# More row maxima among the q projections, a lead stage half as long, and a k-v-gate projection by two products

## The chip, the cores and the metric

The kernel runs on one core of a Trainium2 chip. The metric is the device time of one execution in microseconds; it is 1746.71 us before the change (median of 3 runs, 1746.21 to 1747.7). The engines are PE (matrix products), ACT, DVE and POOL (element-wise work, each with its own queue) and SP, whose queue issues every DMA of this kernel. PE writes to eight PSUM banks, which are named here by their tags: S0 to S4, F0, F1 and V.

## The reference, cut to what matters

```python
a = einsum("bsd,ed->bse", x, dft_hid_re);  b = einsum("bsd,ed->bse", x, dft_hid_im)
y = einsum("ts,bse->bte", dft_seq_re, a) - einsum("ts,bse->bte", dft_seq_im, b)

q = (x @ wq).reshape(B, S, 32, 20).transpose(0, 2, 1, 3)      # 32 heads of 20
k = x @ wk;  v = x @ wv                                       # one k and v for all heads
p = softmax(einsum("bhqd,bkd->bhqk", q, k) * 20 ** -0.5)
o = einsum("bhqk,bkd->bhqd", p, v)  ->  (S, 640) @ wo

g = sigmoid((x * gate_w).sum(-1))
out = g * y + (1 - g) * o
```

S is 2048 and D is 640, all in float32. To hold that precision the kernel splits most operands into a high part (rounded to fp32r) and the rest, the low part, and adds three products: high by high, high by low, low by high.

## The kernel before, in words

**Projection stage.** x comes in four blocks n = 0 to 3 of 512 tokens. Of each block, five chunks c of 128 channels are split into xh (ACT) and xl (DVE). Two things are projected: kv, 41 columns of k, v and the gate (`kv_mm`, `kv_out`), and q, in five tiles m of 128 columns, 15 matmuls of 512 columns each (`q_mm`, `q_out`). `q_out` copies the high part qh from PSUM (ACT), subtracts to get ql (DVE) and sends both to DRAM (qh_d, ql_d); three buffers each rotate. `kv_out` does the same with k and sends it six times into ks; `kv_turn` transposes v and the gate. Block 0 runs chunk by chunk, since the weights wq come in chunks too; blocks 1 to 3 run tile by tile. In block 3, four half maxima follow each of the tiles m = 0 to 3.

**A half maximum** ("a half") is one matmul of 128 queries by 512 keys for one head into a bank (`a_unit`, PE `a<-ks,qs`) and one maximum over the keys from that bank (DVE `mx<-a`). It needs the rows qs of its head, which are read back from qh_d and ql_d (`load_qs`), and ks. 64 half maxima finish a pair of heads, over 1024 queries; the sum over keys can start only after that.

**Lead stage.** 240 puts (a put is one step of a DFT product, on both halves of PE at once) make the first 16 groups of the hidden DFT (`ab`, 15 puts each), with 72 half maxima between them. They use the weights w0 (real part), wb and w1 (imaginary part), each loaded as `wraw` and split on POOL (`load_w`, `split_w`), and tiles of x, loaded as `xraw` (`load_x`) and split by ACT (`xh<-xraw`) and POOL (`xl<-xraw`) in `split_x`. All raw tiles of these two kinds go through one ring of two buffers (`raw_tile`).

**Loop.** 256 rounds. Each has 8 exponentials on ACT (`pt<-b`) with their score matmuls b, 16 matmuls av, in rounds that need it 8 half maxima, and a number of DFT puts. Plan AB15 has 15 puts of the hidden DFT (rounds 0 to 47), Y16 has 16 puts of the sequence DFT (rounds 48 to 191, six products), Y12 has 12 (rounds 192 to 223, the seventh product), and then come output groups and the end. A short tail follows.

**What sets the order.** Orders on PE, ACT, DVE and POOL are those in which the program is written. The DMAs on SP are put in order by a scheduler at build time, and SP then takes them strictly one after the other: a DMA that has to wait holds all that are behind it.

Of the kernel before, what the change touches and what calls it, by code (L numbers as in the profile page):

```python
# [8 lines left out]
F32 = mybir.dt.float32  # L9
# [8 lines left out]
P = 128  # L18
# [15 lines left out]
def kernel(  # L34
# [66 lines left out]
    gate = const.tile([P, NT], F32, name="gate")  # L101
    omg = const.tile([P, NT], F32, name="omg")

    nc.gpsimd.memset(ks.bitcast(F32), 1.0)
    nc.gpsimd.memset(vsb, 1.0)

    nc.scalar.activation(gate, ident[:, :NT], AF.Exp)

# [47 lines left out]
    for t in mxr:
# [69 lines left out]
    mx = {}  # L226
    QB = NT // 2
    UV = 4 * QB

    def a_unit(u, hh, tag="A"):  # L230

        v, r = divmod(u, UV)
        qb, c = divmod(r, 4)
        if r == 0 and v not in mx:
            mx[v] = qsp.tile([P, 2, QB, 4], F32, tag=f"mx{v % 2}", name="mx", bufs=1)
        b = 64 * hh
        ps = bank(tag, f"a_{u}_{hh}")
        nc.tensor.matmul(  # L238
            ps,
            qs[v][b : b + 60, qb * P : (qb + 1) * P],  # L240
            ks[b : b + 60, c * ROW : (c + 1) * ROW],
            start=True,
            stop=True,
        )
        nc.vector.tensor_reduce(mx[v][:, hh, qb, c : c + 1], ps, axis=AX.X, op=ALU.max)  # L245
# [74 lines left out]
    with ExitStack() as c1:  # L320
        w1 = c1.enter_context(tc.tile_pool(name="w1", bufs=1, side="right"))
        x1 = c1.enter_context(tc.tile_pool(name="x1", bufs=2, side="right"))
        rot = Rot(["B", "V", "F", "B", "F", "A", "A", "A"])
        kvg = w1.tile([P, KC, 41], F32, name="kvg")
        kvgh = w1.tile([P, KC, P], F32R, name="kvgh")
        kvgl = w1.tile([P, KC, P], F32R, name="kvgl")
        nc.gpsimd.memset(kvgh.bitcast(F32), 0.0)
        nc.gpsimd.memset(kvgl.bitcast(F32), 0.0)
        wqh = w1.tile([P, KC, D], F32R, name="wqh")
        wql = w1.tile([P, KC, D], F32R, name="wql")  # L330
        wq_v = wq.rearrange("(c p) n -> p c n", p=P)
        xs, xsp = {}, {}

        def load_x1(n, c):
            if n < 4:
                if c == 0:
                    xs[n] = x1.tile([P, KC, ROW], F32, name="xr")
                move(xs[n][:, c], xT_v[:, c, n * ROW : (n + 1) * ROW])

        def split_x1(n, c):  # L340
            if n < 4:
                if c == 0:
                    xh = x1.tile([P, KC, ROW], F32R, name="xh")
                    xl = x1.tile([P, KC, ROW], F32R, name="xl")
                    xsp[n] = (xh, xl)
                xh, xl = xsp[n]
                split(xs[n][:, c], xh[:, c], xl[:, c])

        def q_mm(ps, n, m, c):
            ms = slice(m * P, (m + 1) * P)  # L350
            xh, xl = xsp[n]
            mm3(ps, wqh[:, c, ms], wql[:, c, ms], xh[:, c], xl[:, c], KC, c)

        def q_out(ps, n, m):
            ms, ts = slice(m * P, (m + 1) * P), slice(n * ROW, (n + 1) * ROW)
            qh = x1.tile([P, ROW], F32R, name="qh", bufs=3)
            ql = x1.tile([P, ROW], F32R, name="ql", bufs=3)
            nc.scalar.activation(qh, ps, AF.Copy)
            nc.vector.tensor_tensor(ql, ps, qh.bitcast(F32), op=ALU.subtract)
            move(qh_d[ms, ts], qh)  # L360
            move(ql_d[ms, ts], ql)

        def kv_mm(ps, n, c):
            xh, xl = xsp[n]
            mm3(ps, kvgh[:, c], kvgl[:, c], xh[:, c], xl[:, c], KC, c)

        def kv_out(ps, n):
            ts = slice(n * ROW, (n + 1) * ROW)
            kvT = x1.tile([41, ROW], F32, name="kvT")
            kh = x1.tile([DH, ROW], F32R, name="kh")  # L370
            kl = x1.tile([DH, ROW], F32R, name="kl")
            nc.scalar.activation(kvT, ps[:41], AF.Copy)
            nc.scalar.activation(kh, ps[:DH], AF.Copy)
            nc.vector.tensor_tensor(kl, ps[:DH], kh.bitcast(F32), op=ALU.subtract)
            for r0 in (0, 64):
                move(ks[r0 : r0 + 20, ts], kh)
                move(ks[r0 + 20 : r0 + 40, ts], kl)
                move(ks[r0 + 40 : r0 + 60, ts], kh)
            return kvT

        def kv_turn(kvT, n, rot):
            ps = rot(f"kvt_{n}")
            for j in range(4):
                nc.tensor.transpose(
                    ps[:, 64 * j : 64 * j + 41], kvT[:, j * P : (j + 1) * P], ident[:41, :41]
                )
            pv = ps.rearrange("p (j c) -> p j c", c=64)[:, :4]
            ns = slice(4 * n, 4 * n + 4)
            nc.scalar.activation(vsb[:, ns, :DH], pv[:, :, DH : 2 * DH], AF.Copy)
            nc.vector.tensor_copy(  # L390
                gz[:, ns].rearrange("p (j o) -> p j o", o=1), pv[:, :, 2 * DH : 2 * DH + 1]
            )


        def gate_out():
            nc.vector.tensor_scalar_max(gz, gz, -87.0)
            nc.scalar.activation(omg, gz, AF.Exp, scale=-1.0)
            nc.vector.tensor_scalar_add(omg, omg, 1.0)
            nc.vector.reciprocal(gate, omg)
            nc.vector.tensor_scalar(omg, gate, -1.0, 1.0, op0=ALU.mult, op1=ALU.add)  # L400

        load_x1(0, 0)
        move(kvg, wkvg.rearrange("(c p) n -> p c n", p=P))
        pkv = rot("kv_0")
        pq = [rot(f"q_0_{m}") for m in range(KC)]
        for c in range(KC):
            if c:
                load_x1(0, c)
            raw = w1.tile([P, D], F32, name="wraw", bufs=2)
            move(raw, wq_v[:, c])  # L410
            split_x1(0, c)
            if c == 0:
                split(kvg, kvgh[:, :, :41], kvgl[:, :, :41])
            split(raw, wqh[:, c], wql[:, c])
            kv_mm(pkv, 0, c)
            for m in range(KC):
                q_mm(pq[m], 0, m, c)
        for c in range(KC):
            load_x1(1, c)
        for c in range(KC):  # L420
            split_x1(1, c)
        kvT = kv_out(pkv, 0)
        for m in range(KC):
            q_out(pq[m], 0, m)
        for n in range(1, 4):
            for c in range(KC):
                load_x1(n + 1, c)
            if n == 3:
                rot = Rot(["F1", "V", "S0", "F0", "F1", "V", "S0", "F0"])
            pkv = rot(f"kv_{n}")  # L430
            for c in range(KC):
                kv_mm(pkv, n, c)
            kv_turn(kvT, n - 1, rot)
            kvT = kv_out(pkv, n)
            if n == 3:
                load_qs(0)
                for k in range(2):
                    load_x(k)
                for k in range(2):
                    split_x(k)  # L440
                load_x(2)
            for m in range(KC):
                ps = rot(f"q_{n}_{m}")
                for c in range(KC):
                    q_mm(ps, n, m, c)
                split_x1(n + 1, m)
                q_out(ps, n, m)
                if n == 3 and m < KC - 1:
                    for z in range(4):
                        a_half(z % 2, f"S{1 + z}")  # L450
                    if m == 1:
                        kv_turn(kvT, 3, rot)
                        gate_out()
            if n < 3:
                load_w(n - 1, 0)
                split_w(n - 1)
# [563 lines left out]

    LEAD = 12
    NL = 2 * (UV + LEAD)
    KL = 15 * 2 * SJ
    done = first = 2 * state[0]
    for n in range(1, KL + 1):
        y_put(1)
# [10 lines left out]
    stage["loop"] = True  # L1037

    ROUNDS = [(p, qh, kk) for qh in range(2) for p in range(NPAIR) for kk in range(NT // 2)]
    NAB = 3 * 2 * SJ  # L1040
    Y3 = 48

    NO = len(ROUNDS) - NT * 2

    def plan_of(n):
        if n < NAB or NO <= n < NO + NT:
            return AB15
        if n < NAB + 3 * Y3:
            return Y16
        if n >= len(ROUNDS) - 2:  # L1050
            return N0
        return Y12 if state[1] < NA else N12
# [95 lines left out]
```

## Time and profile before

| | us |
|---|---|
| median of three runs | 1746.71 |
| the profiled execution | 1745.61 |
| its span | 1743.8 |
| projection stage (0 to 99.9) | 99.9 |
| lead stage (99.9 to 145.6) | 45.7 |
| loop, 256 rounds (145.6 to 1719.8) | 1574.2 |
| tail | 24.0 |

The granted clock of the profiled execution is 0.998. PE is busy for 99% of the span, DVE 78%, ACT 73%, POOL 63%. A window row gives a stretch's length, then each engine's busy time and instructions, the granted PE clock, the DMA share and GB/s. A timeline row gives start, length, engine, source line, operation, out<-in, shapes and count, and in brackets how long the engine sat idle before and what ended that.

### The profile page before, as it was taken

To read this page: it belongs to the slowest core of one execution; us is meant where nothing else is said; L and a number is where in the kernel's file an instruction comes from. 1 tells how busy PE (TensorE), PEld (TensorE's weight loads), DVE (VectorE), ACT (ScalarE), POOL (GpSimd) and SP (SyncE) were. 2 spreads that over 40 slices of the span, in tenths; PEclk is the share of its full clock that TensorE was granted. 3 is DMA by queue.
4 is the path that set the end of the run, shared out by engine and by line. 5 is a ranking of instruction groups with operands and counts; after the bars stand their busy time and mean duration, and the time that the engine had idled before them with its cause. 6 is when DMAs were issued, how large, how long until landed. Compare 5 with 4: busy or idle time off the path is not lost.

```text
span 1743.8 us, 43691 instructions
## 1 busy us (share of the span) xinstructions
PE 1723.9 (99%) x16754; PEld 1230.0 (71%) x16754; DVE 1363.0 (78%) x2285; ACT 1270.6 (73%) x2556; POOL 1095.9 (63%) x910
## 2 busy tenths in 40 slices
PE   8999999999999999999999999999999999999997
PEld 6797777777777677777777777777777666667664
DVE  4498888888887888888888888888888888888823
ACT  3337887878767777777777777777777777788895
POOL 4056563333788555577778888888877453357784
PEclk9999999999999999999999999999999999999999
DMA  7652232222777533466667775555555232234332
GB/s 247 189 168 88 67 109 86 67 71 71 236 222 237 181 104 114 136 194 231 222 200 226 243 229 173 194 188 175 172 168 155 88 102 73 63 109 123 102 92 84
DMA packets 181322, 261.49 MB, mean 150 GB/s; under 512 B 35636, under 2 KB 136244, under 8 KB 181112
## 3 DMA queue, kind: packets, MB, share of 16 engines
q1 hardware_dynamic: 181112, 258.70, 47.3%
q8 instruction: 131, 2.15, 0.5%
q14 instruction: 79, 0.65, 0.1%
HBM read 184.42 MB, written 76.99 MB: 150 GB/s over the span
## 4 chain that ended last, share of the span: by engine, by line
PE 92%; DVE 3%; DMA 2%; SPq 1%; issue 1%; ACT 1%; POOL 0%; POOLq 0%; DVEq 0%; ACTq 0%
PE av L934 27%; PE y_p L742 19%; PE b L922 19%; PE a L238 15%; PE ab L742 6%; PE oo L742 3%; DVE mx L245 2%; SPq L113 1%; PE q L121 1%; PE q L123 1%; PE q L122 1%; DMA wraw<-in_wq_dram 1%; DMA qh_d<-qh 0%; DVE xl L117 0%; DMA xr<-in_xT_dram 0%
## 5 line engine op out<-in xcount | busy, mean ns | idle before, releaser
L245 DVE TENSOR_REDUCE mx<-a 128x1 f32<-128x512 f32 x2048 | 1277.6, 684 | 260.7 <-PE a L238 234.1
L930 ACT ACTIVATE pt<-b 128x512 f32<-128x512 f32 x2048 | 1073.1, 605 | 337.2 <-PE a L238 269.3
L922 PE MATMUL b<-qs,ks 62*128 62x512 f32 x2048 | 762.0, 413 | 3.4 <-ACT pt L930 1.4
L238 PE MATMUL a<-ks,qs 60*128 60x512 f32 x2048 | 719.2, 409 | 0.5 <-DVE mx L245 0.4
L742 PE MATMUL y_p<-tb,ch 64*128 64x320 f32 x3584 | 633.4, 306 | 0.0
L922 PEld LDWEIGHTS b<-qs,ks 62*128 62x128 f32 x2048 | 346.3, 185 | 225.2 <-DVE mx L245 155.2
L934 PE MATMUL av<-pt,vsb 128*32 128x512 f32 x4096 | 492.3, 598 | 0.0
L742 PEld LDWEIGHTS y_p<-tb,ch 64*128 64x128 f32 x3584 | 480.0, 185 | 9.0
L742 PE MATMUL y_p<-tb,cl 64*128 64x320 f32 x1792 | 444.9, 306 | 0.0
L238 PEld LDWEIGHTS a<-ks,qs 60*128 60x128 f32 x2048 | 350.6, 185 | 7.3 <-issue 1.1
L784 POOL TENSOR_TENSOR yt<-yt,yu 128x320 f32<-128x320 f32 x86 | 74.8, 870 | 336.3 <-ACT yu L779 307.0
L742 PEld LDWEIGHTS y_p<-tb,cl 64*128 64x128 f32 x1792 | 274.6, 185 | 5.7
L503 POOL TENSOR_TENSOR cl<-craw,ch 128x1024 fp32r<-128x1024 f32 x112 | 268.0, 2393 | 9.0
L934 PEld LDWEIGHTS av<-pt,vsb 128*32 128x32 f32 x4096 | 107.0, 109 | 224.8 <-issue 215.5
L784 POOL TENSOR_TENSOR abt<-abt,abu 128x320 f32<-128x320 f32 x64 | 55.8, 872 | 183.3 <-ACT abu L779 175.8
L497 POOL TENSOR_TENSOR craw<-craw 128x1024 f32<-128x1024 f32 x64 | 153.8, 2403 | 0.0
L502 POOL CAST ch<-craw 128x1024 fp32r<-128x1024 f32 x112 | 116.3, 1038 | 13.8 <-DMA braw<-b_d 7.4
L742 PE MATMUL oo<-wo,osp 64*128 64x320 f32 x816 | 92.9, 307 | 0.0
L742 PEld LDWEIGHTS oo<-wo,osp 64*128 64x128 f32 x816 | 87.4, 185 | 1.6
L529 POOL TENSOR_TENSOR tb<-braw,tb 128x320 fp32r<-128x320 f32 x80 | 68.4, 876 | 0.0
L742 PE MATMUL ab<-wbh,xh 64*128 64x320 f32 x256 | 59.0, 307 | 0.0
L742 PE MATMUL ab<-wbh,xl 64*128 64x320 f32 x256 | 58.3, 305 | 0.0
(138 smaller groups left out, 1614.2 us busy)
## 6 DMA issues: line engine op xcount, KB each, us to landing
craw<-in_cre_dram SPq DMA_DIRECT2D x80, 512.0 KB
craw<-in_cim_dram SPq DMA_DIRECT2D x64, 512.0 KB
s_d<-craw SPq DMA_DIRECT2D x32, 512.0 KB
craw<-s_d SPq DMA_DIRECT2D x32, 512.0 KB
braw<-b_d SPq DMA_DIRECT2D x80, 160.0 KB
xraw<-in_xT_dram SPq DMA_DIRECT2D x32, 320.0 KB
qs<-qh_d SPq DMA_DIRECT2D x128, 80.0 KB
b_d<-abt SPq DMA_DIRECT2D x64, 160.0 KB
```

The costliest lines, as they stand in the source:

```text
L113: nc.sync.dma_start(words(dst), words(src))
L238: nc.tensor.matmul(ps, qs[v][b : b + 60, qb * P : (qb + 1) * P], ks[b : b + 60, c * ROW : (c + 1) * ROW], start=True, stop=True,)
L245: nc.vector.tensor_reduce(mx[v][:, hh, qb, c : c + 1], ps, axis=AX.X, op=ALU.max)
L497: nc.gpsimd.tensor_tensor(raw[0], raw[0], raw[1], op=how)
L502: nc.gpsimd.tensor_copy(h, raw[0])
L503: nc.gpsimd.tensor_tensor(l, raw[0], h.bitcast(F32), op=ALU.subtract)
L529: nc.gpsimd.tensor_tensor(t[:, 1], raw, t[:, 0].bitcast(F32), op=ALU.subtract)
L742: nc.tensor.matmul(ps, w, x, start=start, stop=stop)
L784: nc.gpsimd.tensor_tensor(t0, t0, t1, op=ALU.add)
L922: nc.tensor.matmul(ps, ks[b : b + 62, kc * P : (kc + 1) * P], qs[NPAIR * (qc // 2) + p][b : b + 62, (qc % 2) * ROW : (qc % 2 + 1) * ROW], ...
L930: nc.scalar.activation(t, ps, AF.Exp, scale=SCALE)
L934: nc.tensor.matmul(ps[32 * g : 32 * g + 32, :], vsb[:, kc, :], t, start=first, stop=last)
```

## The change

- **k, v and gate by two products.** The high and the low part of the weights stand side by side in one stationary tile kvgs (columns 0 to 40 and 64 to 104). One matmul per chunk by xh makes high by high and low by high at once, in two groups of PSUM rows; a second one by xl uses the first 41 columns. `kv_out` adds the two groups: ACT copies the low rows (kvl), DVE adds (kvT), ACT makes kh and DVE kl.
- **Start.** Nine matmuls of 128 columns on the identity are issued before anything else on PE. The memsets of ks and vsb come after that of kvgs.
- **xl of blocks 2 and 3** is subtracted on POOL and no longer on DVE.
- **Banks.** From block 1 on, the projections rotate over four banks (F1, V, S0, F0), so that S1 to S4 are free for the half maxima.
- **Half maxima.** qs of the first pair of heads is loaded block by block (`load_qs0`), the half maxima go in key order (`EARLY`), and four follow each of the tiles m = 2, 3 of block 1 and all five of blocks 2 and 3: 48 rather than 16 in the projection stage.
- **Lead and loop.** The lead stage has 120 puts (8 groups) and 40 half maxima. The other 8 groups go into the loop: AB15 in rounds 0 to 55, Y16 in rounds 56 to 223, and no Y12 for the seventh product.

```diff
+    warm = bank("S4", "warm")
+    for _ in range(9):
+        nc.tensor.matmul(warm[:, :P], ident, ident, start=True, stop=True)
...
+    EARLY = [(qb, 0) for qb in range(4)] + [(qb, 0) for qb in range(4, QB)]
+    EARLY += [(qb, c) for c in range(1, 4) for qb in range(QB)]
...
-        rot = Rot(["B", "V", "F", "B", "F", "A", "A", "A"])
+        rot = Rot(["S1", "S0", "F0", "S2", "S3", "S4", "F1", "V", "S0", "F0"])
...
-                split(xs[n][:, c], xh[:, c], xl[:, c])
+                nc.scalar.activation(xh[:, c], xs[n][:, c], AF.Copy)
+                (nc.gpsimd if n > 1 else nc.vector).tensor_tensor(
+                    xl[:, c], xs[n][:, c], xh[:, c].bitcast(F32), op=ALU.subtract
+                )
...
-            mm3(ps, kvgh[:, c], kvgl[:, c], xh[:, c], xl[:, c], KC, c)
+            end = c == KC - 1
+            for high in (not end, end):
+                m, x = (105, xh) if high else (41, xl)
+                nc.tensor.matmul(ps[:m], kvgs[:, c, :m], x[:, c], start=(c == 0 and high), stop=(end and high))
...
-            nc.scalar.activation(kvT, ps[:41], AF.Copy)
-            nc.scalar.activation(kh, ps[:DH], AF.Copy)
-            nc.vector.tensor_tensor(kl, ps[:DH], kh.bitcast(F32), op=ALU.subtract)
+            nc.scalar.activation(kvl, ps[64:105], AF.Copy)
+            nc.vector.tensor_tensor(kvT, ps[:41], kvl, op=ALU.add)
+            nc.scalar.activation(kh, kvT[:DH], AF.Copy)
+            nc.vector.tensor_tensor(kl, kvT[:DH], kh.bitcast(F32), op=ALU.subtract)
...
+        load_qs0(0)
+        rot = Rot(["F1", "V", "S0", "F0"])
+        slots = {1: (2, 3), 2: range(KC), 3: range(KC)}
...
-            if n == 3:
-                rot = Rot(["F1", "V", "S0", "F0", "F1", "V", "S0", "F0"])
...
-                load_qs(0)
...
-                if n == 3 and m < KC - 1:
+                if (n, m) == (1, 0):
+                    load_qs0(1)
+                if m in slots[n]:
                     for z in range(4):
                         a_half(z % 2, f"S{1 + z}")
...
-    KL = 15 * 2 * SJ
+    KL = 15 * SJ
...
-    NAB = 3 * 2 * SJ
-    Y3 = 48
+    NAB = 7 * SJ
+    NY = 3 * SJ * len(PRODUCTS)
```

The queue of SP changes although no line says so. Before, the loads of the imaginary weights (wiT) and of the first two x tiles of the lead stage (xraw) stand among the loads of the first blocks (xr), ahead of everything that block 0 sends:

```order
L113 DMA wraw<-in_wiT_dram 128x3x320
L113 DMA wraw<-in_wiT_dram 128x2x320
L113 DMA wraw<-in_wq_dram 128x640
L113 DMA xr<-in_xT_dram 128x512 x5
L113 DMA xraw<-in_xT_dram 128x5x128 x2
L113 DMA xr<-in_xT_dram 128x512 x5
L113 DMA ks<-kh 20x512
```

Now they stand behind the last q tile that block 2 sends, and the ks of block 3:

```order
L114 DMA qh_d<-qh 128x512
L114 DMA ql_d<-ql 128x512
L114 DMA wraw<-in_wiT_dram 128x3x320
L114 DMA wraw<-in_wiT_dram 128x2x320
L114 DMA ks<-kh 20x512
L114 DMA ks<-kl 20x512
L114 DMA ks<-kh 20x512 x2
L114 DMA ks<-kl 20x512
L114 DMA ks<-kh 20x512
L114 DMA xraw<-in_xT_dram 128x5x128 x2
L114 DMA qs_119<-qh_d 20x1024 x2
```

What moved are two transfers of weights and two of x, past some 55 other DMAs.

On POOL the splits of both sets of weights stood together, ahead of the x tiles:

```order
L200 CAST w0h<-wraw 128x960
L201 TENSOR_TENSOR w0l<-wraw,w0h 128x960
L200 CAST wbh_500<-wraw 128x640
L201 TENSOR_TENSOR wbl_501<-wraw,wbh_500 128x640
L200 CAST w1h<-wraw 128x960
L201 TENSOR_TENSOR w1l<-wraw,w1h 128x960
L200 CAST wbh<-wraw 128x640
L201 TENSOR_TENSOR wbl<-wraw,wbh 128x640
L316 TENSOR_TENSOR xl<-xraw,xh 128x640 x2
```

Now the subtractions of blocks 2 and 3 stand around the first set:

```order
L361 TENSOR_TENSOR xl<-xr,xh 128x512 x5
L211 CAST w0h<-wraw 128x960
L212 TENSOR_TENSOR w0l<-wraw,w0h 128x960
L211 CAST wbh_539<-wraw 128x640
L212 TENSOR_TENSOR wbl_540<-wraw,wbh_539 128x640
L361 TENSOR_TENSOR xl<-xr,xh 128x512 x5
L211 CAST w1h<-wraw 128x960
L212 TENSOR_TENSOR w1l<-wraw,w1h 128x960
L211 CAST wbh<-wraw 128x640
L212 TENSOR_TENSOR wbl<-wraw,wbh 128x640
L329 TENSOR_TENSOR xl<-xraw,xh 128x640 x2
```

The order of the weights and the x tiles among themselves is the same; five subtractions are ahead of the first set and five between the two.

On ACT, at the start of block 3, the two copies `xh<-xraw` stand ahead of the copies qh of that block's q tiles, as they did before:

```order
L372 ACTIVATE kvT<-kv_683 41x512
L373 ACTIVATE kh<-kv_683 20x512
L315 ACTIVATE xh<-xraw 128x640 x2
L358 ACTIVATE qh<-q_0_740 128x512
L358 ACTIVATE qh<-q_1_775 128x512
```

and now:

```order
L394 ACTIVATE kh<-kvT 20x512
L328 ACTIVATE xh<-xraw 128x640 x2
L374 ACTIVATE qh<-q_0_833 128x512
L374 ACTIVATE qh<-q_1_867 128x512
L410 ACTIVATE vsb<-kvt_901 128x4x20
```

Here nothing moved but the copy of k, which now follows the sum kvT on DVE; q_0 and q_1 are the first two q tiles of block 3.

More of the change, by code (lines that the diff above doesn't have):

```diff
@@ L102 @@
     omg = const.tile([P, NT], F32, name="omg")
-    nc.gpsimd.memset(ks.bitcast(F32), 1.0)
-    nc.gpsimd.memset(vsb, 1.0)
+    warm = bank("S4", "warm")
+    for _ in range(9):
+        nc.tensor.matmul(warm[:, :P], ident, ident, start=True, stop=True)
     nc.scalar.activation(gate, ident[:, :NT], AF.Exp)
@@ L153, in load_qs, with load_qs0 @@
             move(t[b + 40 : b + 60], ql_d[r, ts])
+    def load_qs0(n):
+        if n == 0:
+            qs[0] = qbuf[0]
+        ts = slice(n * ROW, (n + 1) * ROW)
+        for hh in range(2):
+            r = slice(hh * DH, (hh + 1) * DH)
+            for k, src in enumerate((qh_d, qh_d, ql_d)):
+                b = 64 * hh + 20 * k
+                move(qs[0][b : b + 20, ts], src[r, ts])
     mxr = [qsp.tile([P, 32], F32, name=f"mxr{i}") for i in range(2)]
@@ L228 @@
     UV = 4 * QB
+    EARLY = [(qb, 0) for qb in range(4)] + [(qb, 0) for qb in range(4, QB)]
+    EARLY += [(qb, c) for c in range(1, 4) for qb in range(QB)]
     def a_unit(u, hh, tag="A"):
         v, r = divmod(u, UV)
-        qb, c = divmod(r, 4)
+        qb, c = EARLY[r] if v == 0 else divmod(r, 4)
         if r == 0 and v not in mx:
@@ L322 @@
         x1 = c1.enter_context(tc.tile_pool(name="x1", bufs=2, side="right"))
-        rot = Rot(["B", "V", "F", "B", "F", "A", "A", "A"])
+        rot = Rot(["S1", "S0", "F0", "S2", "S3", "S4", "F1", "V", "S0", "F0"])
         kvg = w1.tile([P, KC, 41], F32, name="kvg")
[L325 to L328, printed above, removed]
+        kvgs = w1.tile([P, KC, P], F32R, name="kvgs")
+        nc.gpsimd.memset(kvgs.bitcast(F32), 0.0)
+        nc.gpsimd.memset(ks.bitcast(F32), 1.0)
+        nc.gpsimd.memset(vsb, 1.0)
         wqh = w1.tile([P, KC, D], F32R, name="wqh")
@@ L369, in kv_out @@
             kvT = x1.tile([41, ROW], F32, name="kvT")
+            kvl = x1.tile([41, ROW], F32, name="kvl", bufs=1)
             kh = x1.tile([DH, ROW], F32R, name="kh")
             kl = x1.tile([DH, ROW], F32R, name="kl")
-            nc.scalar.activation(kvT, ps[:41], AF.Copy)
-            nc.scalar.activation(kh, ps[:DH], AF.Copy)
-            nc.vector.tensor_tensor(kl, ps[:DH], kh.bitcast(F32), op=ALU.subtract)
+            nc.scalar.activation(kvl, ps[64:105], AF.Copy)
+            nc.vector.tensor_tensor(kvT, ps[:41], kvl, op=ALU.add)
+            nc.scalar.activation(kh, kvT[:DH], AF.Copy)
+            nc.vector.tensor_tensor(kl, kvT[:DH], kh.bitcast(F32), op=ALU.subtract)
             for r0 in (0, 64):
@@ L410 @@
             move(raw, wq_v[:, c])
+            if c == 0:
+                nc.vector.tensor_copy(kvgs[:, :, :41], kvg)
+                nc.vector.tensor_tensor(
+                    kvgs[:, :, 64:105], kvg, kvgs[:, :, :41].bitcast(F32), op=ALU.subtract
+                )
             split_x1(0, c)
-            if c == 0:
-                split(kvg, kvgh[:, :, :41], kvgl[:, :, :41])
             split(raw, wqh[:, c], wql[:, c])
@@ L447 @@
                 q_out(ps, n, m)
-                if n == 3 and m < KC - 1:
+                if (n, m) == (1, 0):
+                    load_qs0(1)
+                if m in slots[n]:
                     for z in range(4):
                         a_half(z % 2, f"S{1 + z}")
-                    if m == 1:
-                        kv_turn(kvT, 3, rot)
-                        gate_out()
+                if (n, m) == (3, 1):
+                    kv_turn(kvT, 3, rot)
+                    gate_out()
             if n < 3:
@@ L1047, in plan_of @@
             return AB15
-        if n < NAB + 3 * Y3:
+        if n < NAB + NY:
             return Y16
```

## The prediction, made before the changed kernel had run

> **What bounds the kernel now.** I read the busy shares first, then the span by stages (columns: length, then PE, PEld, DVE, ACT and POOL busy), then the stages' timelines.
>
> ```profile
> PE 1723.9 (99%) x16754; PEld 1230.0 (71%) x16754; DVE 1363.0 (78%) x2285; ACT 1270.6 (73%) x2556; POOL 1095.9 (63%) x910
> ...
> 0.00:30.70 30.70, 23.86 (x91) 18.48 (x92) 14.54 (x15) 12.73 (x23) 17.49 (x24) 1.00 0.78 250
> ...
> 74.50:99.90 25.40, 25.40 (x116) 18.33 (x114) 14.70 (x28) 5.88 (x12) 3.08 (x2) 1.00 0.47 151
> 99.90:145.60 45.70, 45.18 (x558) 44.53 (x559) 44.62 (x77) 23.08 (x56) 36.34 (x37) 1.00 0.48 147
> ```
>
> The average says PE. In the projection of blocks 1 to 3 that holds: PE has no gap, DVE has room. In the lead stage PE and DVE are both full (45.18 and 44.62 of 45.70). DVE's row there is one unbroken run of maxima, 28.96 / 48 = 0.603 us each, so PE's fullness is partly a pace that DVE sets:
>
> ```profile
> 101.33 28.96 DVE L245 TENSOR_REDUCE mx<-a 128x1 f32<-128x512 f32 x48
> ```
>
> The loop is read by its exponentials, 8 to a round, in the stretches of plan AB15, Y16 and Y12:
>
> ```profile
> 145.60:440.80 295.20, 203.66 (x384) 1.00 0.26 78
> 440.80:1345.40 904.60, 597.62 (x1152) 1.00 0.60 191
> 1345.40:1539.20 193.80, 137.79 (x256) 1.00 0.27 81
> ```
>
> A round of AB15 takes 295.20 / 48 = 6.150 us, of Y16 904.60 / 144 = 6.282, of Y12 193.80 / 32 = 6.056. Four more puts cost 0.22 us: in a round a put is cheap, since the round's maxima and exponentials are there anyway.
>
> **Loop.** 32 rounds of Y12 become 8 of AB15 and 24 of Y16: 8 × 6.150 + 24 × 6.282 − 32 × 6.056 = **+6.2**. Bounds 5 to 8, the upper one if the longer Y16 part, which moves 191 GB/s, meets its own transfers.
>
> **Start of the projection.** Block 0 waits for weights: PE stood 5.71 us at the start and 0.28 + 0.84 in chunk 2.
>
> ```profile
> 5.71 0.79 PE L121 MATMUL kv<-xh,kvgh 128*128 128x512 f32 x1 [5.71 <-ACT kvgh L116]
> ...
> 10.57 0.40 PE L123 MATMUL q<-xh,wql 128*128 128x512 f32 x1
> ...
> 17.54 0.50 PE L121 MATMUL q<-xh,wqh 128*128 128x512 f32 x1 [0.28 <-ACT wqh L116]
> ...
> 19.12 0.50 PE L123 MATMUL q<-xh,wql 128*128 128x512 f32 x1 [0.84 <-DVE wql L117]
> ...
> 16.75 0.74 ACT L116 ACTIVATE wqh<-wraw 128x640 fp32r<-128x640 f32 x1 [7.13 <-DMA wraw<-in_wq_dram]
> ...
> 17.52 1.54 DVE L117 TENSOR_TENSOR wql<-wraw,wqh 128x640 fp32r<-128x640 f32 x1 [7.17 <-ACT wqh L116]
> ```
>
> The nine warm-up matmuls and the missing kv product shorten chunks 0 and 1, but chunk 2 still starts when its wq has landed and is split. That load is one place earlier on SP, ahead of 320 KB that take 1.3 us at the window's 250 GB/s; I take 0.9. The subtraction wql, 1.54 us while POOL splits weights, has POOL idle beside it now; I take half its time off, 0.7. Chunks 3 and 4 save two matmuls of 0.233: **−2.1** (−1 to −3). The pace of the first eleven matmuls, (10.57 − 5.71) / 11 = 0.44, is covered by that wait.
>
> **Products of k, v and gate.** A 512-column matmul starts every (77.90 − 74.64) / 14 = 0.233 us; blocks 1 to 3 save 15: **−3.5**. The extra DVE addition per block has cover where DVE idles (14.70 busy of 25.40).
>
> ```profile
> 74.64 0.39 PE L121 MATMUL kv<-xh,kvgh 128*128 128x512 f32 x1
> ...
> 77.90 0.39 PE L123 MATMUL kv<-xh,kvgl 128*128 128x512 f32 x1
> ...
> 82.28 0.73 PE L238 MATMUL a<-ks,qs 60*128 60x512 f32 x4
> ...
> 86.64 0.73 PE L238 MATMUL a<-ks,qs 60*128 60x512 f32 x4
> ...
> 83.63 2.47 DVE L245 TENSOR_REDUCE mx<-a 128x1 f32<-128x512 f32 x4
> ```
>
> **Half maxima among the q tiles.** A tile with four half maxima takes 86.64 − 82.28 = 4.36 us, one without 15 × 0.233 = 3.50; eight more tiles have them: 8 × 0.86 = **+6.9**. On DVE each costs 2.47 us for the four maxima and 0.69 for ql (`75.47`, below), 3.2 of 4.36 us, so it keeps up; the ten subtractions that leave for POOL find it empty between the splits of weights.
>
> **Lead stage.** 72 maxima become 40: 32 × 0.603 = **−19.3**. PE's side is lower: 120 puts and 40 half maxima are half and 56% of what filled 45.18 us, about 24, against DVE's 26.4. If PE were the sole bound it would be −21.
>
> **Block 1.** Four banks rotate now, so q tile 2 takes the bank of kv_1, which is free when ACT and DVE have made kvl and kvT. Those stand behind the last q tiles of block 0, and these wait for buffers, that is for qh_d to land:
>
> ```profile
> 31.57 2.24 SPq L113 DMA_DIRECT2D xr<-in_xT_dram  x5
> 33.91 0.91 SPq L113 DMA_DIRECT2D ks<-kh  x1
> ...
> 38.84 0.42 SPq L113 DMA_DIRECT2D qh_d<-qh  x1
> ...
> 41.44 0.60 ACT L358 ACTIVATE qh<-q 128x512 fp32r<-128x512 f32 x1 [10.24 <-DMA qh_d<-qh]
> 43.45 0.60 ACT L358 ACTIVATE qh<-q 128x512 fp32r<-128x512 f32 x1 [1.41 <-DMA qh_d<-qh]
> ```
>
> Before, nothing on PE needed that in time. Now PE wants the bank when block 0, kv_1 and two tiles are through: 30.7 − 2.1 + 10 × 0.233 + 0.4 + 7.0 = 38.3. On SP the loads of xraw and of the last x block no longer stand ahead, so I put the first ks at 27.9 and qh_d at 27.9 + 4.93 = 32.8; the landings follow 2.6 and 4.6 us later as in the rows, then 0.6 (qh), 0.7 (ql), 0.6 and 0.7 (kvl, kvT): 39.8 to 40. Stall 1.5, and 0.3 for the first half maxima behind the round trip of qs: **+1.8** (0 to 5).
>
> **Block 3.** This is the term that decides. The raw tiles use a ring of two, and the order is wiT, wiT, xraw, xraw. Before, wiT left SP at 18.41 and xraw at 26.06, some 50 us ahead of need; ACT copied xraw without a wait.
>
> ```profile
> 18.41 3.62 SPq L113 DMA_DIRECT2D wraw<-in_wiT_dram  x2
> ...
> 26.06 2.93 SPq L113 DMA_DIRECT2D xraw<-in_xT_dram  x2
> ...
> 22.12 1.02 POOL L200 CAST w1h<-wraw 128x960 fp32r<-128x960 f32 x1 [0.51 <-DMA wraw<-in_wiT_dram]
> ...
> 26.55 2.04 POOL L201 TENSOR_TENSOR wbl<-wraw,wbh 128x640 fp32r<-128x640 f32 x1
> ...
> 74.40 0.40 PE L123 MATMUL q<-xh,wql 128*128 128x512 f32 x1
> ...
> 79.78 1.35 ACT L315 ACTIVATE xh<-xraw 128x640 fp32r<-128x640 f32 x2
> 82.39 0.60 ACT L358 ACTIVATE qh<-q 128x512 fp32r<-128x512 f32 x1 [1.26 <-PE q L123]
> ...
> 75.47 0.69 DVE L359 TENSOR_TENSOR ql<-q,qh 128x512 fp32r<-128x512 f32 x1 [2.21 <-ACT qh L358]
> ```
>
> Now wiT stands behind ql_d of block 2's last tile. Let T be the start of that tile's last matmul (74.40 in the rows). ql ends 1.8 later, so wiT leaves at T + 2.1. By the rows it is used 22.12 − 18.41 = 3.7 after that, and POOL ends the four steps of the splits (26.55 + 2.04) − 22.12 = 6.5 later: T + 12.3. Only then is the second buffer free and the second xraw leaves; with the same 3.7 it lands at T + 16.1. ACT waits for it with `xh<-xraw`, and behind that stand the copies qh of block 3. So xh ends at T + 16.9, qh of tile 0 at 17.4, ql at 18.1, its four maxima at 20.6. The half maxima of tile 1 need the banks of those of tile 0, one after the other, so their last goes at T + 20.6. PE wants it at (86.64 − 74.40) − 5 × 0.233 + 0.86 + 3 × 0.15 = T + 12.4: **+8.2** (0 to 9). PE idles for about 6 of these.
>
> **Clock.** What PE loses after a gap is seen at the end of the kernel: after 1.96 us of idling (and 0.21 a little later) the pace goes from (1726.80 − 1724.74) / 14 = 0.147 to (1734.26 − 1731.06) / 12 = 0.267 for 12 matmuls, 1.4 us.
>
> ```profile
> 1724.74 0.31 PE L121 MATMUL o_late<-wo,osp 128*128 128x320 f32 x1
> ...
> 1726.80 0.31 PE L123 MATMUL o_late<-wo,osp 128*128 128x320 f32 x1
> 1729.07 0.42 PE L121 MATMUL o<-wl,osp 128*128 128x320 f32 x1 [1.96 <-ACT osp L980]
> ...
> 1731.06 0.47 PE L121 MATMUL o<-wl,osp 128*128 128x320 f32 x1
> ...
> 1734.26 0.33 PE L121 MATMUL o<-wl,osp 128*128 128x320 f32 x1
> ```
>
> I take **+1.4** after block 3's gap (0 to 2.3, what the start's eleven slow matmuls lost, 11 × 0.21). [...]
>
> **Sum.** To the first exponential −2.1 − 3.5 + 6.9 − 19.3 + 1.8 + 8.2 + 1.4 = −6.6, with the loop's +6.2 **−0.4**. The profiled execution takes 1745.61 (span 1743.8 and 1.8 around it), 1.1 below the median, so this is 1745.2 for it and about **1746** for the median.
>
> **Rivals.**
> - *The hold in block 3 is absent or short.* For it: the chain goes through five queues, and each step is taken at the pace of another place. Against it: order and ring are fixed, and the price has two transfers and four splits in a row. Without the stall and its clock, −0.4 − 9.6 = −10.0: 1736.7. With half of it, 1741.5.
> - *Slower, by kv_1's bank.* If qh_d leaves SP no earlier than before, at 38.84, kvT comes at 45.5 to 46 and PE stalls some 7.4 rather than 1.5: 1752.2. It makes the kernel slower by over 0.2% from qh_d at about 37. For it: SP is strictly in order and had the x loads of 2.24 us ahead. Against it: the kv result is ready 2 us sooner.
> - *The loop takes the puts worse than the rows say* (upper bound 8): 1748, still within 0.2%.
> - *The change doesn't do what it says:* if two products don't shorten kv because a 105-row product takes longer, −3.5 goes: 1749.8. Nothing speaks for it; the cost in the rows goes by the columns.
>
> **How the numbers follow.** 0.2% is 3.5 us, about what a measurement of this kernel tells from no change. Forecast 0.50; hold absent 0.15, halved 0.13; bank 0.10; loop 0.08; kv 0.04. The forecast's own range is 1742 to 1750. Faster by over 0.2% (below 1743.2): 0.15 + 0.10 of the halved case + 0.09 of the forecast = 0.34. Slower (above 1750.2): 0.09 of the bank + 0.04 of the forecast + 0.03 of the last two = 0.16. Same: 0.50. The range goes from 1737.5 to 1750.5, which leaves some 0.1 at each end.
>
> **What would show it.** In the changed profile: first exponential near 139, or near 130 if the hold is absent; `xh<-xraw` at the start of block 3 idle about 10 us before it on the DMA of xraw; PE idle about 6 us before a half maximum on `mx`; a stall of 1 to 2 us in block 1; maxima at 0.6 us through a lead stage of about 27 us; loop rounds at 6.15 and 6.28. The forecast is wrong if ACT reaches qh of block 3 without waiting, or if the rounds change pace.

## The result, and the profile after

| | before | changed |
|---|---|---|
| median, us (20 runs each, same chip) | 1746.45 | 1750.71 |
| lowest to highest | 1744.56 to 1748.04 | 1748.04 to 1753.89 |
| profiled: span | 1743.8 | 1749.4 |
| profiled: first put of the lead | 99.94 | 113.16 |
| profiled: first exponential | 145.64 | 142.07 |
| profiled: loop (first exponential to the last round's end) | 1574.2 | 1583.4 |

The changed kernel is **slower**, by 0.23%: ratio 1.0023, interval 1.0016 to 1.003. The forecast was no change, 1746 in a range of 1737.5 to 1750.5.

The changed kernel in four windows, which hold most of block 1, of block 2, of block 3 and the lead (columns as before). The first matmuls of blocks 1, 2 and 3 stand at 28.81, 53.69 and 78.24:

```profile
28.50:52.00 23.50, 21.42 (x93) 15.19 (x92) 8.80 (x15) 8.01 (x16) 5.15 (x5) 1.00 0.75 218
52.00:76.00 24.00, 24.00 (x107) 16.81 (x107) 16.50 (x28) 7.05 (x13) 13.07 (x10) 1.00 0.64 191
76.00:110.00 34.00, 26.96 (x111) 18.21 (x110) 16.61 (x32) 6.27 (x12) 8.74 (x6) 0.85 0.55 155
112.40:142.10 29.70, 26.88 (x288) 25.45 (x286) 27.84 (x49) 11.66 (x29) 17.14 (x18) 0.94 0.33 104
```

The window from 76 to 110 shows the loss: PE lacks 7 us of 34 and its granted clock is 0.85. Its timeline, engine by engine along the forecast's chain (SP, POOL, ACT, DVE, PE):

```profile
79.45 0.98 SPq L114 DMA_DIRECT2D wraw<-in_wiT_dram  x2
...
88.23 1.81 SPq L114 DMA_DIRECT2D xraw<-in_xT_dram  x2
...
83.81 1.19 POOL L211 CAST w1h<-wraw 128x960 fp32r<-128x960 f32 x1 [8.01 <-DMA wraw<-in_wiT_dram]
...
88.08 1.56 POOL L212 TENSOR_TENSOR wbl<-wraw,wbh 128x640 fp32r<-128x640 f32 x1
...
91.51 0.74 ACT L328 ACTIVATE xh<-xraw 128x640 fp32r<-128x640 f32 x1 [8.07 <-DMA xraw<-in_xT_dram]
93.51 0.74 ACT L328 ACTIVATE xh<-xraw 128x640 fp32r<-128x640 f32 x1 [1.27 <-DMA xraw<-in_xT_dram]
94.27 1.09 ACT L374 ACTIVATE qh<-q 128x512 fp32r<-128x512 f32 x2
...
94.90 0.69 DVE L375 TENSOR_TENSOR ql<-q,qh 128x512 fp32r<-128x512 f32 x1 [10.75 <-ACT qh L374]
...
96.25 2.58 PE L251 MATMUL a<-ks,qs 60*128 60x512 f32 x4 [7.04 <-DVE mx L258]
...
99.35 0.63 PE L123 MATMUL q<-xl,wqh 128*128 128x512 f32 x1
...
101.91 0.41 PE L123 MATMUL q<-xl,wqh 128*128 128x512 f32 x1
```

wiT leaves late, the splits follow, the second xraw leaves when wbl's split has ended, ACT waits 8.07 + 1.27 us for the two, and PE idles 7.04 us for a bank. Then, from 99.35 to 101.91, six matmuls run at 0.43. In the loop, two rounds stand out: round 60 takes 6.86 us and round 63 takes 9.07, by the first exponentials of consecutive rounds. In round 63 PE waits for the transfer that adds the maxima to qs. The maxima m are complete at 518.9, and m_d, which sends them, leaves SP at 535.31:

```profile
540.08 0.47 PE L948 MATMUL b<-qs,ks 62*128 62x512 f32 x1 [2.76 <-DMA qs<-m_d]
...
518.70 0.22 DVE L273 TENSOR_REDUCE m<-m 128x32 fp32r<-128x64 f32 x1
...
530.50 1.75 SPq L114 DMA_DIRECT2D braw<-b_d  x4
...
535.31 1.22 SPq L114 DMA_DIRECT2D m_d<-m  x2
538.35 0.55 SPq L114 DMA_DIRECT2D qs<-m_d  x2
```

### The profile page after: what moved, and what is told of

It reads as the page before. It is cut to its first block, busy times and chain, and to the rows that moved or that the text cites. A ratio compares the mean times of both kernels' runs of the same rounds, so it can differ in the third digit from the quotient of the medians.

```text
span 1749.4 us, 43682 instructions
## 1 busy us (share of the span) xinstructions
PE 1717.4 (98%) x16752; PEld 1223.0 (70%) x16752; DVE 1359.8 (78%) x2280; ACT 1261.8 (72%) x2543; POOL 1113.6 (64%) x931
## 4 chain that ended last, share of the span: by engine, by line
PE 93%; DVE 2%; DMA 2%; ACT 1%; POOL 1%; SPq 0%; issue 0%; POOLq 0%; DVEq 0%; ACTq 0%
PE av L960 27%; PE y_p L768 19%; PE b L948 19%; PE a L251 15%; PE ab L768 7%; PE oo L768 3%; DVE mx L258 1%; PE q L122 1%; PE q L124 1%; PE q L123 1%; SPq L114 0%; ACT pt L956 0%; DMA wraw<-in_wq_dram 0%; DMA xr<-in_xT_dram 0%; DMA wraw<-in_wiT_dram 0%
## 5 line engine op out<-in xcount | busy, mean ns | idle before, releaser
L948 PE MATMUL b<-qs,ks 62*128 62x512 f32 x2048 | 750.2, 408 | 6.5 <-DMA qs<-m_d 2.8
L251 PE MATMUL a<-ks,qs 60*128 60x512 f32 x2048 | 704.6, 409 | 10.6 <-DVE mx L258 9.4
```

The lines of the kernel that those rows point to most:

```text
L251: nc.tensor.matmul(ps, qs[v][b : b + 60, qb * P : (qb + 1) * P], ks[b : b + 60, c * ROW : (c + 1) * ROW], start=True, stop=True,)
L948: nc.tensor.matmul(ps, ks[b : b + 62, kc * P : (kc + 1) * P], qs[NPAIR * (qc // 2) + p][b : b + 62, (qc % 2) * ROW : (qc % 2 + 1) * ROW], ...
```

## Experiments

My theory after the comparison: the hold in block 3 costs about 9.6 us as forecast; the lead is DVE's chain of maxima and gave less than forecast; the loop costs the forecast's 6 us, and a further wait for `qs<-m_d`. Ratios are against the kernel before, on the same chip.

**e1: the hold taken away.**

```diff
-                for k in range(2):
-                    split_x(k)
-                load_x(2)
...
+                if (n, m) == (3, 3):
+                    for k in range(2):
+                        split_x(k)
+                    load_x(2)
```

> The changed kernel, but the first two x tiles of the lead stage are split after q tile 3 of block 3 rather than ahead of tile 0, so that ACT's copies qh no longer stand behind the wait for xraw. Theory (the hold in block 3 costs 8.2 us plus 1.4 us of slow clock): PE's gap of 7.4 us before the half maxima of tile 1 is gone, all matmuls of block 3 run at 0.23, the first exponential comes 9 to 10 us earlier, near 132.5, and the time is about 1741, 5 us below the kernel before. Rival (the lead stage is paced by DVE's maxima, so a later start of it is given back there): the gap goes but the first exponential moves by less than 3 us, and the time stays above 1747.

Measured: 1738.95 us, ratio 0.9956 (0.9943 to 0.9968); first exponential at 131.34, 10.7 earlier than in the changed kernel. Block 3 has no gap and the full clock, and ACT copies the two x tiles without a wait. In the windows of e1 for block 3 and the lead:

```profile
77.70:102.40 24.70, 24.70 (x115) 17.39 (x115) 17.77 (x33) 5.95 (x13) 8.99 (x6) 1.00 0.57 181
102.40:131.30 28.90, 26.13 (x284) 24.95 (x280) 27.77 (x49) 11.21 (x28) 17.08 (x18) 0.94 0.46 148
```

The hold is shown: 0.6 us of the 10.7 stood already at the start of block 3, and block 3 itself is 10.1 shorter, for a forecast price of 9.6. The lead takes 28.9 us in both kernels, so nothing is given back there. The rival falls. This version is 7.3 us faster than the kernel before.

**e9: the cause of the hold.** Why did the order of SP change? The raw buffers are freed by POOL's splits, and the change put the ten subtractions xl among them.

```diff
-                (nc.gpsimd if n > 1 else nc.vector).tensor_tensor(
+                nc.vector.tensor_tensor(
```

> The changed kernel, but the subtractions xl of blocks 2 and 3 stay on DVE, as before the change. POOL then splits the weights at the start, the two raw buffers come free early, and wiT and the first two xraw stand at the front of SP's queue again; ACT's order is that of the changed kernel. Theory (the hold is made by the move of those ten subtractions, through the ring of raw buffers): ACT copies xraw without a wait, PE's gap of 7.4 us goes, DVE holds 0.69 + 0.69 + 2.47 = 3.9 of 4.36 us per tile, first exponential 131.5 to 133, time 1738 to 1741.5. Rival (DVE needs POOL's help with 48 half maxima): the gap goes, but PE waits for xl or the maxima in blocks 2 and 3, 3 us or more, 1743 or later.

Measured: 1744.47 us, ratio 0.9991 (0.9982 to 1.0); first exponential 137.74. SP's queue has wiT and the first two xraw at the front again, and the hold is gone:

```profile
90.06 1.35 ACT L328 ACTIVATE xh<-xraw 128x640 fp32r<-128x640 f32 x2
91.65 0.60 ACT L374 ACTIVATE qh<-q 128x512 fp32r<-128x512 f32 x1 [0.24 <-ACT xh L328]
```

So the move of xl makes the hold. But the time is 3 us above the upper end of the expectation, and not by the rival's way: blocks 2 and 3 run with hardly a gap (0.28 us). The loss lies in block 0 and at the bank of kv_1 (waits of PE):

```profile
16.70 0.50 PE L122 MATMUL q<-xh,wqh 128*128 128x512 f32 x1 [1.74 <-ACT wqh L117]
19.15 0.80 PE L124 MATMUL q<-xh,wql 128*128 128x512 f32 x1 [1.72 <-DVE wql L118]
...
45.77 0.77 PE L122 MATMUL q<-xh,wqh 128*128 128x512 f32 x1 [2.94 <-DVE kvT L393]
```

The wait of 1.74 stands in the changed kernel too (1.75 at 16.88). The one of 1.72 does not: POOL splits the first set of weights from 15.12 on in e9 and is idle there in the changed kernel, and DVE's wql beside it takes 2.42 us against 0.83. First e9, then the changed kernel:

```profile
16.68 2.42 DVE L118 TENSOR_TENSOR wql<-wraw,wqh 128x640 fp32r<-128x640 f32 x1 [6.41 <-ACT wqh L117]
```

```profile
16.86 0.83 DVE L118 TENSOR_TENSOR wql<-wraw,wqh 128x640 fp32r<-128x640 f32 x1 [6.58 <-ACT wqh L117]
```

After 19.15 a dozen matmuls run at 0.43. The wait at 45.77 is the forecast's slower rival, at its place and by its cause: with wiT and xraw ahead on SP the first ks leaves at 33.76 (27.60 in the changed kernel), qh of block 0 is held until 43.30 for qh_d to land, kvl and kvT follow. Moving xl to POOL thus had two sides: it freed the start and made the hold in block 3.

**e2 and e3: lead and loop apart.** e2 is the changed kernel with the old lead and loop, e3 the old kernel with the new ones.

```diff
-    KL = 15 * 2 * SJ
+    KL = 15 * SJ
...
-    NAB = 3 * 2 * SJ
-    Y3 = 48
+    NAB = 7 * SJ
+    NY = 3 * SJ * len(PRODUCTS)
...
-        if n < NAB + 3 * Y3:
+        if n < NAB + NY:
```

(e3 has this diff, e2 its reverse on the changed kernel.)

> The changed kernel with the lead stage and the loop plan of before (240 puts in the lead, 48 rounds of AB15, seventh product in rounds of Y12). Theory (the lead is then bound by PE: 45.2 us of before less 32 half maxima at 0.15): lead about 40.4 instead of 29.5, first exponential near 153, loop back to 1574, with neither the dearer rounds (6.2) nor the stall in round 63 (3): 1751 to 1753. Rival (it is the move of 120 puts into the loop that made the kernel slow): the time falls below the one before, to 1745 or less.

> The kernel before with only the last part of the change: 120 puts in the lead, the other 8 groups in the loop; projection, banks and 72 maxima in the lead as before. Theory (DVE paces the lead: 72 maxima at 0.603 and 2.4 us around them): lead 45 to 46 as before, loop +6.2, and +3 more if the stall of round 63 comes with the later start of Y16: 1752.5 to 1756. Rival (PE was the bound of the lead): lead shorter by 8 us or more, time 1745 or less.

Measured: e2 1757.05 us, ratio 1.0061 (1.0047 to 1.0074); e3 1752.21, ratio 1.0034 (1.0021 to 1.0047). Their leads, e2's and then e3's:

```profile
113.50:156.10 42.60, 40.94 (x526) 40.30 (x524) 31.20 (x49) 22.69 (x56) 36.02 (x37) 1.00 0.43 135
```

```profile
99.60:144.70 45.10, 43.63 (x314) 30.49 (x313) 44.02 (x77) 11.67 (x29) 17.28 (x18) 1.00 0.32 97
```

With 72 maxima, half the puts save 0.7 us (45.7 to 45.0): the lead was DVE's, and the same 120 puts cost 7.2 in the loop (1581.4 against 1574.2). With the 40 half maxima of the new lead they save 13.7 (42.6 to 28.9). So the move of the puts is right only together with the move of the maxima, and in the changed kernel it is worth 13.7 less the loop's 6 to 9. e2's time is 4 over the upper end of the expectation, 2.2 of it in the lead. Its loop is 1573.8, as before.

**e4 and e12: the four maxima of the last tile.** Both drop the half maxima after tile 4 of block 3, in the changed kernel and in e1.

```diff
-        slots = {1: (2, 3), 2: range(KC), 3: range(KC)}
+        slots = {1: (2, 3), 2: range(KC), 3: range(KC - 1)}
```

> The changed kernel, but no half maxima after the last q tile of block 3, so that the lead has 44 and not 40. Theory (those four maxima are worked off by DVE inside the lead anyway, so they belong to its 44 x 0.603): the first exponential comes about 0.9 us earlier, near 141.2, since PE leaves block 3 that much sooner. Rival (only the 40 of the lead count, as the forecast had it): four maxima more there, 2.4 later less 0.9, near 143.6.

> As e1, without half maxima after the last q tile of block 3. Theory (the lead is a chain of DVE's maxima that starts at the last ql): first exponential 0.5 to 0.9 us earlier than in e1, as e4 against the changed kernel, time within 1 us of e1's 1739. Rival (four more maxima in the lead): 1.5 later.

Measured: e4 has its first exponential at 141.42 (0.65 earlier) and 1750.37 us in one run; e12 at 130.87 (0.47 earlier) and 1739.35. The rival would have had them 1.5 later. Four maxima that are issued after the last tile are worked off in the lead anyway: the changed kernel, e1, e4 and e12 all have 44 maxima on DVE between the first put and the first exponential. In the changed kernel six maxima in a row begin on DVE at the last ql's end, and only then does it idle:

```profile
113.38 0.69 DVE L375 TENSOR_TENSOR ql<-q,qh 128x512 fp32r<-128x512 f32 x1 [1.28 <-ACT qh L374]
113.99 3.67 DVE L258 TENSOR_REDUCE mx<-a 128x1 f32<-128x512 f32 x6
117.99 0.69 DVE L258 TENSOR_REDUCE mx<-a 128x1 f32<-128x512 f32 x1 [0.33 <-PE a L251]
```

**e10: the two products alone**, on the kernel before.

```diff
-            mm3(ps, kvgh[:, c], kvgl[:, c], xh[:, c], xl[:, c], KC, c)
+            end = c == KC - 1
+            for high in (not end, end):
+                m, x = (105, xh) if high else (41, xl)
+                nc.tensor.matmul(ps[:m], kvgs[:, c, :m], x[:, c], start=(c == 0 and high), stop=(end and high))
...
-            nc.scalar.activation(kvT, ps[:41], AF.Copy)
-            nc.scalar.activation(kh, ps[:DH], AF.Copy)
-            nc.vector.tensor_tensor(kl, ps[:DH], kh.bitcast(F32), op=ALU.subtract)
+            nc.scalar.activation(kvl, ps[64:105], AF.Copy)
+            nc.vector.tensor_tensor(kvT, ps[:41], kvl, op=ALU.add)
+            nc.scalar.activation(kh, kvT[:DH], AF.Copy)
+            nc.vector.tensor_tensor(kl, kvT[:DH], kh.bitcast(F32), op=ALU.subtract)
```

> The kernel before with only the two products for k, v and gate (one stationary tile, sum in kv_out). Theory (15 matmuls of 0.233 less in blocks 1 to 3, the ones of block 0 partly behind the wait for weights): first exponential 3.5 to 4.2 us earlier, near 141.8, loop as before, time 1742 to 1743. Rival (the 105-row product or the longer chain kvl, kvT, kh, kl gives it back): less than 1.5 us.

Measured: 1755.91 us, ratio 1.0053 (1.0039 to 1.0066): **10 us slower**, and neither theory had that. First exponential 155.99. PE's wait in block 2, and SP and ACT ahead of it:

```profile
57.90 0.65 PE L366 MATMUL kv<-xl,kvgs 128*41 128x512 f32 x1 [5.17 <-DVE xl L117]
...
52.52 0.32 SPq L113 DMA_DIRECT2D qh_d<-qh  x1
...
55.37 0.60 ACT L356 ACTIVATE qh<-q 128x512 fp32r<-128x512 f32 x1 [4.36 <-DMA qh_d<-qh]
```

The chain kvl, kvT, kh, kl is longer; the six ks transfers leave 1.8 us later (47.37, as kh ends, against 45.59 before), behind them qh_d (52.52 against 50.76), and ACT waits for its landing with xh of the next block behind it. About half of the 1.8 is older: ks of block 0 already leaves 0.9 later (34.78 against 33.91), since one x load holds SP for 1.4 us. Before, PE waited 0.61 us at this point, so the chain had no slack; the wait of 5.17 is that chain, 1.9 later, and PE, which now comes 2.7 earlier.

The larger loss comes behind it. At the start of block 3 e10 is 3.3 us late (77.92 against 74.64), at the first put 10.3. A wait of 5.50 us stands before a half maximum in block 3. The profile names nothing that ended it, but a low part of qs is loaded at 87.76, behind the six ks of that block, where it stood ahead of them before (76.55), and PE goes on 2.6 us after that. A slow clock goes with both waits: 0.85 in the window from 52 to 75, 0.86 in that from 75 to 100. What the two products are worth in the changed kernel, where the x loads no longer stand ahead on SP, was not measured apart. The products themselves cost what was said, 0.233 each at 105 and at 41 rows (the first rows of block 2 in the changed kernel):

```profile
53.69 0.39 PE L384 MATMUL kv<-xh,kvgs 128*105 128x512 f32 x1
53.92 0.39 PE L384 MATMUL kv<-xl,kvgs 128*41 128x512 f32 x1
54.15 0.40 PE L384 MATMUL kv<-xh,kvgs 128*105 128x512 f32 x1
```

**e7: no warm-up matmuls.**

```diff
-    warm = bank("S4", "warm")
-    for _ in range(9):
-        nc.tensor.matmul(warm[:, :P], ident, ident, start=True, stop=True)
```

> The changed kernel without the nine matmuls on the identity. Theory (chunk 2 waits for its weights either way): the first matmuls run at 0.43, PE's gap ahead of chunk 2 shrinks from 2.1 us to under 1, and the first exponential and the time stay within 0.5 us of the changed kernel. Rival (they bring the clock up for good): 2 us later, 1752.7.

Measured: 1749.5 us (1745.57 to 1751.42 over 10 runs; ratio 1.0014, 1.0005 to 1.0022), first exponential at 143.10 against the changed kernel's 142.07. The time shows no gain from the warm-up; the profile has 1.0 us, more than the 0.5 expected, and PE's wait for kv_1's bank is as much longer (1.93 against 0.91). The first ten matmuls run at 0.43, and the gap ahead of chunk 2 is gone, so the wait for weights covers the slow start, as the theory said.

**e5: the stalls of block 1.**

```diff
-        slots = {1: (2, 3), 2: range(KC), 3: range(KC)}
+        slots = {1: (3, 4), 2: range(KC), 3: range(KC)}
...
-            pkv = rot(f"kv_{n}")
+            pkv = bank("S1", "kv_1") if n == 1 else rot(f"kv_{n}")
```

> As e1, with kv of block 1 in bank S1 instead of the four rotating ones, and the half maxima of block 1 after tiles 3 and 4 instead of 2 and 3. Theory (block 1 stalls for kv_1's bank, 0.9 us, and for the first rows of qs, 1.1): both gaps of PE go, the first exponential comes about 2 us earlier than in e1, near 129.3, and the time is near 1737. Rival (the stall moves on, to the next tile's bank or to a later arrival of qs): the first exponential gains less than 0.8 us.

Measured: 1742.64 us, ratio 0.9977 (0.9967 to 0.9988), 3.7 over e1; first exponential 135.59. Both waits of block 1 are gone, and one of 3.31 us stands at its end. The half maxima after tile 4 need the banks of those after tile 3, whose maxima stand on DVE behind a ql, and that waits for its buffer:

```profile
52.53 0.69 DVE L375 TENSOR_TENSOR ql<-q,qh 128x512 fp32r<-128x512 f32 x1 [7.57 <-DMA ql_d<-ql]
```

The rival is right that the stall moves on, though to a third place: PE ran ahead into the wait for SP's transfers of ql in block 1 and lost more there. Behind the wait the first matmuls of block 2 run at 0.43 (56.94 to 59.50).

**e6, e8, e11: the wait in round 63.** e6 starts Y16 two rounds earlier, e8 adds e5's edit, e11 makes the maxima earlier.

```diff
-    KL = 15 * SJ
+    KL = 15 * 10
...
-    NAB = 7 * SJ
-    NY = 3 * SJ * len(PRODUCTS)
+    NAB = 54
+    NY = 162
```

```diff
-    LEAD = 12
+    LEAD = 13
```

> As e1, with 10 groups (150 puts) in the lead, 54 rounds of AB15, 162 of Y16 and 8 of Y12. Theory (the stall in round 63 is SP's lateness in the first 50 us of Y16, where the transfer of the next maxima stands at its end): Y16 now begins two rounds ahead of a change of heads, the transfer of round 63 comes 12 us further on in the stretch, and round 63 takes 6.3. The loop is 1.5 shorter by its plan and 0.5 by that round, the lead 0 to 1 longer: 1736.5 to 1738.5. Rival (the stall belongs to that pair of heads and not to the start of the stretch): round 63 stays at 6.5 to 7.4.

> The edits of e5 and e6 together. Theory (they act in different stages): their gains add, 1734.5 to 1736.5. Rival (what is gained before the lead is given back in it): as the better of the two, 1737.

> As e1, with the half maxima running two more ahead of their heads (13 units instead of 12), so that each set is complete 1.5 us earlier in the loop, with the DMAs of SP in the same order. Theory (round 63's stall is SP reaching the transfer late, not DVE finishing late): the offset of the transfer qs<-m_d in the first Y16 stretch and the stall of round 63 stay, 6.5 to 7.4. Rival (the maxima come late): round 63 takes 6.3. The lead has two more maxima, 1.2 us.

Measured: e6 1742.91 us, ratio 0.9977 (0.9968 to 0.9987); e8 1745.34, ratio 0.9996 (0.9986 to 1.0007); e11 1738.66 in one run. The place of the transfer in SP's queue against round 63, over the kernels whose Y16 starts at 56 (offset of the issue of `qs<-m_d` from the first exponential of round 56, and the lengths of rounds 60 and 63, from the profiles):

| | offset, us | round 60, us | round 63, us |
|---|---|---|---|
| e4 | 48.36 | 6.39 | 6.55 |
| e1 | 48.50 | 6.26 | 6.82 |
| e11 | 48.62 | 6.78 | 6.56 |
| e9 | 49.00 | 6.42 | 7.36 |
| e5 | 49.39 | 6.99 | 6.93 |
| e3 | 49.50 | 6.89 | 7.42 |
| e12 | 49.50 | 6.70 | 7.48 |
| e7 | 50.75 | 6.70 | 8.60 |
| changed kernel | 51.28 | 6.86 | 9.07 |

The kernel before has 47.94 for its round 55, which takes 6.28, and 6.27 in round 52. So the margin is zero at about 48 plus what PE itself was late by round 60, and what SP is late beyond that, round 63 loses: in the changed kernel 51.28 − 48 − 0.59 = 2.7, for 9.07 − 6.27 = 2.8; in e5 49.39 − 48 − 0.72 = 0.7, for 0.7. In all nine rows the two agree to 0.3. e11 did not do what it was built for: the set of maxima for round 63 is complete 31.7 us after the first exponential of round 56, against 31.3 in e1, so it is no earlier. But the profiles settle the question without it. The maxima are complete at 31 to 32 in all nine and m_d leaves SP only at 45.6 to 48.2: it is SP, which has them in its queue some 14 to 16 us. In e6 the wait in round 63 is gone (6.26), as expected, but another wait for a transfer stands in round 76, which takes 11.1: DVE waits for the sums of a finished head, and PE for DVE.

```profile
607.59 0.25 DVE L988 RECIPROCAL rc<-sm 128x16 f32<-128x16 f32 x1 [4.39 <-DMA sm<-sum_d]
...
608.44 0.50 PE L251 MATMUL a<-ks,qs 60*128 60x512 f32 x1 [2.85 <-DVE mx L258]
```

So e6 loses 4 us against e1. The wait in round 76 doesn't come with the plan alone: e8 has the same plan, both its rounds 63 and 76 take 6.27, and its loop, 1579.7, is the shortest of those with 120 or 150 puts in the lead. But e8 has e5's wait at the end of block 1 again (3.67 us) and is slower than e5 and e6, so no gains add up. The kernel before has the wait for the sums too, in round 68 (7.16). Why SP is late by a varying amount in the first rounds of Y16 isn't settled: the offset differs by up to 3 us between kernels that are alike there, and e10, whose loop is that of before, had 49.56. In the two latest, the changed kernel and e7, it arises at one place: the first of the four braw<-b_d ahead of m_d (530.50 in the rows of the changed kernel) waits for t_d<-braw to land and leaves at an offset of 43.4 and 43.3, in the other seven at 40.3 to 41.1. Why that landing is late is open.

## Why the prediction was wrong, point by point

- **Block 3, right.** Forecast: last half maximum of tile 1 at T + 20.6, a loss of 8.2, and 1.4 for the clock. Measured: T is 77.2 (ql of block 2's last tile ends 1.8 after it, at 79.0), the last of the four matmuls, 0.6 apart, goes at 96.25 + 3 × 0.6 = 98.05, T + 20.8. The six slow matmuls lose 6 × 0.2 = 1.2, near the 1.4 taken from the tail's row; the clock itself was at half for longer (0.50 in the window from 91.7 to 101.9), but for most of that PE stood or went at the pace of the maxima. The single steps were less exact than their sum: wiT was used 4.4 us after its issue (3.7 said), the splits took 5.8 (6.5), the first xraw 3.3 (3.7).
- **Block 1, right in place, small in size.** Stalls of 0.91 and 1.09 us idle, 2.9 in all with the paced half maxima, for a forecast of 1.8. (Block 1 takes 24.9 us; block 2, without a stall, takes 24.55 with three more tiles of half maxima at 0.86.)
- **Start of the lead, right, in part by luck.** Forecast 99.94 + 12.7 = 112.6, measured 113.16. The 1.1 us that block 1 took more is made up in block 2: there the kernel before had lost about 1 us at its wait of 0.61, the changed kernel has no such wait, and the forecast had not counted it.
- **Lead, wrong: one of the two steps that failed.** Forecast −19.3, measured 28.9 − 45.7 = −16.8. I counted the lead's maxima as 40 by the program, but the lead is DVE's chain, and DVE's window has 49 instructions where there were 77: 28 maxima less, not 32. The four of the last q tile, which the change adds, fall into the lead; in the kernel before, tile 4 had none. The statement "DVE keeps up" was right for all tiles but the last. That 4 × 0.603 = 2.4 is so near the 2.5 that are missing is partly chance. The leads of e5 and e9, with the same 44 maxima and a granted clock of 1.00, take 28.0; those of the changed kernel, e1 and e7, with 0.94, take 28.9. So 0.9 of the 2.5 is slow clock after the lead's wait of 1.55, for which the forecast had no term, and the maxima account for about 1.6: 2.4 less 0.6, since DVE's first maximum now follows the first put by 0.83 us and not by 1.39, and 0.2 that stay open.
- **Loop, right by plan and wrong in sum: the other step that failed.** The forecast +6.2 is e1's loop to 0.1 us (1580.4 − 1574.2), by chance to that degree: e1 has a stall of 0.5 in round 63, and the kernel before one of 0.9 in round 68 that e1 hasn't. The changed kernel's profiled loop is +9.2, 3.0 over the forecast, and the wait for `qs<-m_d` in round 63 is 2.8; the other profiles with Y16 from round 56 have +6.2 to +8.4. The upper bound of 8 allowed for transfers in the way, but the sum put that wait at nothing: the place, a transfer with no margin, was not named, and I took the kernel before for one in which it had some.
- **Sum.** −0.4 + 2.5 (lead) + 0.5 (start of the lead) + 3.0 (loop) = +5.6, what the profiled spans show (1749.4 − 1743.8). The medians differ by 4.3: the profiled execution of the kernel before is 0.8 below its median, that of the changed kernel 0.5 above. That the loop's wait varies from run to run would fit, but each kernel has one profile, so it isn't shown. The hold in block 3, the term that decides, was the forecast one; the lead saved less and the loop cost more than said, and the range had no room above for both.
- **The rivals.** The hold's absence, 1736.7, is e1 within 2.3 us. The bank of kv_1 cost 2.9 us of waiting in e9, where xraw again stood ahead. The rival "a 105-row product takes longer" is false: 0.233 each at 105 and at 41 rows. But the sentence that the extra addition "has cover where DVE idles" looked at DVE's busy share alone: in e10 SP's transfers stand behind the longer chain and leave later.

## What to carry to other kernels

A step that is moved from one engine to another can move a buffer's release, with it the order of a queue that no line of the change mentions, and so hold an engine in a later stage, here PE for 7.04 us in block 3: follow the buffers, not only the engines. Count a stage's work by the engine that paces it, from where that engine stands when the stage begins, not by the program's lines. A wait of 0.6 us for a chain means that the chain has no slack: in e10 its transfers left 1.8 us later, PE's wait ended 1.9 later, and a granted clock of 0.85 came on top.

## What the runs showed that I had not expected

- Two products instead of three, alone, made the kernel 10 us slower (e10), though each matmul saved is worth its 0.233. Some 7 of the 10 come in block 3, where a load of qs had moved behind six other transfers on SP.
- PE's clock fell after short waits, but not after each: in e9 waits of 1.74 and 1.72 us were followed by a dozen matmuls at 0.43 (granted clock 0.89 in the window from 0 to 31), while in the changed kernel the wait of 1.75 alone, at 16.88, left the pace at 0.233. The lead's wait of 1.55 or 1.56 us was followed by a granted clock of 0.94 in the changed kernel, e1 and e7, and of 1.00 in e5, e9 and e11; in e1 the clock is 0.50 from 105.2 to 108.6. So the length of the one wait doesn't decide it.
- The subtraction wql on DVE took 2.42 us in e9 while POOL split weights, and 0.83 in the changed kernel with POOL idle.
- A transfer of the loop that PE waits for had next to no margin in the kernel before: an offset of 47.94 cost it nothing in round 55, and e1's 48.50 cost 0.5. No wait in its profile shows this; a wait that is just missed leaves no row.
